# A kernel's head, written in a new order: local attention with a feed-forward layer on one Trainium2 core

## The chip, the core and the metric

The kernel runs on one core of a Trainium2 chip. The core has a matrix engine (TensorE, PE in the profile), three engines for element-wise work (VectorE or DVE, ScalarE or ACT, GpSimd or POOL) and SyncE (SP), which here only issues transfers. TensorE writes into PSUM, a small memory of banks, and VectorE and ScalarE read the banks out. Each engine works through its own instructions in order; semaphores tie the engines together. The metric is device microseconds of the whole program, less being better.

## The reference

q, k and v are 4 batches x 8 heads x 768 positions x 64. Each position attends to the 96 positions up to itself and to the first 8, with a bias that falls with distance; then a feed-forward layer with softplus follows.

```python
scores = scale * np.matmul(q, k.transpose(0, 1, 3, 2))
keep = is_global | is_local
bias = -slopes[:, None, None] * dist[None, :, :]
scores = np.where(keep, scores + bias[None], -1000000000.0)
a = np.exp(scores - np.max(scores, axis=-1, keepdims=True))
a = a / (np.sum(a, axis=-1, keepdims=True) + 1e-09)
x = np.matmul(a, v)      # then to 3072 x 512
h = x @ w_in             # 512 x 2048
g = np.maximum(h, 0.0) + np.log1p(np.exp(-np.abs(h)))
out = g @ w_out          # 2048 x 512
```

## The kernel before

**Tiling.** The 24 blocks of 128 queries are taken in units of two neighbouring blocks (`UNITS`, L175); a block sees its own keys and those of the block before it. Two blocks, 256 tokens, form a group of the feed-forward layer; there are 12 groups.

**A unit of attention** goes through named operations. In each name the first number is the unit or the block. `ldq`, `ldk`, `ldv` load (units 0 to 2 load q and k in two halves, `.0` and `.1`, L478); `castq`, `castk`, `castv` turn float32 into bfloat16 (L521 to L551; v in four pieces); `trq`, `trk` transpose q and k, on TensorE for units 0 to 2 (L629) and by a transposing DMA after that (L649, L658); `cpq`, `cpk` copy the transposed halves out of PSUM (L642). For a block n, `sc` makes the scores (L709, L764), on top of a bias that `sb` wrote for blocks 0 and 1, while for the others `z` adds the bias on VectorE (L790); `ex` takes the exponential on ScalarE (L795); `pv` multiplies by v (L821); `nm` divides by the sums on VectorE (L832, L833); `xt` transposes the result, by TensorE for blocks 0 to 5, with `xc` copying it into `XT` (L856, L861), and by a transposing DMA after that (L864). `gk` and `gv` copy the keys and values of the first 8 positions into the slots of the block before (L671, L680).

**A group of the feed-forward layer** has eight slots `a` g.0 to g.7 (`mm1`, L879; each is 8 matmuls of 128x256, and slots 2i and 2i+1 need the w_in pieces 2i and 2i+1), each followed by an exponential `e` on ScalarE (L896), and every two by a logarithm `ln` (L907), so that softplus is ln(1 + exp(h)). The even slots use PSUM bank h0, the odd ones h1. For groups 0 and 1 the second product is `b` g.ns.z (`mm2`, L927), two matmuls of 128x512 for each pair of the 16 rows blocks, with z from 0 to 14; `oc` copies it out and `st` stores it. From group 2 on a scheme of seven products with sums of tokens (`ka`) and of weights (`ws`, L354, on VectorE or GpSimd) replaces it.

**Weights.** `win` 0 to 7 and `wout` 0 to 7 load pieces of 512 KB, `cin` and `cout` cast them (L507). A cast that the code calls for any engine can be put on GpSimd, VectorE or ScalarE; what reads PSUM can be on VectorE or ScalarE.

**Buffers for loads.** There are 12 slots of raw data. They are given out in the fixed order of `FIRST_LOADS` (L178), whatever the order of issue: k0, q0, v0, q1, k1, v1, six pieces of w_in; then win7 takes the slot of k0, win6 that of q0, k2 that of v0, q2 that of q1, w_out 0 and 1 those of two w_in pieces, and so on. A load waits until the casts of what lay in its slot before are done, and behind it on SP's queue wait all later loads. From unit 3 on a load also waits for a slot of the feed-forward layer (L1268): q of unit 3 for a0.6, k for a1.0.

**The order.** It is written by hand in the string `ORDER` (L81): name, colon, engine (P, V, A, G, S), and after @ the PSUM home (s0 and s1 are of two banks, x, o, h0, h1 of one). `Program.in_order` (L63) emits the operations in just this order; so on each engine they stand in the order of the string, and everything else is waits that follow from what an operation reads and writes. A wait holds up all that stands behind it on that engine. `fill` 0 to 25 (L1024) are matmuls on a tile of zeros into bank x whose result nobody reads.

## Time and profile before

| | us |
|---|---|
| median of 3 runs | 210.27 |
| lowest and highest | 209.52, 210.4 |
| span of the profiled execution | 207.6 |
| median less that span | 2.7 |

The trace is of one execution; its span runs from the first to the last instruction. The profiled execution's own time is not given beside its span, so the 2.7 us are the distance to the median of the runs.

| stage of the trace, us | TensorE busy | VectorE | ScalarE | GpSimd | DMA share |
|---|---|---|---|---|---|
| 6.15 to 29.57 | 20.16 of 23.42 | 18.16 | 21.71 | 12.88 | 1.07 |
| 29.57 to 60.19 | 30.17 of 30.62 | 24.55 | 29.53 | 18.95 | 0.97 |
| 60.19 to 207.6 | 143.27 of 147.41 | 120.40 | 126.63 | 88.25 | 0.72 |

A row of a timeline has the start, the length, the engine, the line of the kernel, the instruction, what it writes and reads, the shapes and the number of instructions merged; brackets hold the idle time before it and what ended it. Matmuls are pipelined: the ends are modelled and overlap the next start, so a group's true share of TensorE is the distance of starts. SPq and ACTq are rows of a queue that issues transfers. A transfer's row has its size and the time from issue to landing.

### The profile page before, as it was taken

To read this page: it belongs to the slowest core of one execution; us is meant where nothing else is said; L and a number is where in the kernel's file an instruction comes from. 1 tells how busy PE (TensorE), PEld (TensorE's weight loads), DVE (VectorE), ACT (ScalarE), POOL (GpSimd) and SP (SyncE) were. 2 spreads that over 40 slices of the span, in tenths; PEclk is the share of its full clock that TensorE was granted. 3 is DMA by queue.
4 is the path that set the end of the run, shared out by engine and by line. 5 is a ranking of instruction groups with operands and counts; after the bars stand their busy time and mean duration, and the time that the engine had idled before them with its cause. 6 is when DMAs were issued, how large, how long until landed. Compare 5 with 4: busy or idle time off the path is not lost.

```text
span 207.6 us, 5574 instructions
## 1 busy us (share of the span) xinstructions
PE 198.6 (96%) x2174; PEld 161.1 (78%) x2174; DVE 166.3 (80%) x327; ACT 180.7 (87%) x271; POOL 123.3 (59%) x129
## 2 busy tenths in 40 slices
...
GB/s 185 345 347 384 393 370 364 258 229 190 293 134 245 190 239 242 252 228 231 205 196 224 204 94 229 148 139 244 218 190 27 129 87 33 0 53 102 52 74 133
DMA packets 69115, 41.00 MB, mean 198 GB/s; under 512 B 30432, under 2 KB 61664, under 8 KB 69088
## 3 DMA queue, kind: packets, MB, share of 16 engines
...
q8 instruction: 17, 0.28, 0.6%
...
## 4 chain that ended last, share of the span: by engine, by line
PE 74%; ACT 12%; DMA 8%; DVE 2%; issue 1%; ACTq 0%; SPq 0%; DVEq 0%
PE h_ps L879 24%; PE s_ps L417 12%; PE o_ps L417 9%; PE x_ps L417 5%; PE h_ps L1133 4%; DMA raw<-in_moe_w_in_dram 4%; PE s_ps L927 3%; PE s_ps L1133 3%; PE s_ps L764 3%; PE x_ps L821 3%; ACT e L896 3%; DMA XT<-xs 2%; ACT pb L795 2%; PE o_ps L927 2%; DMA raw<-in_q_dram 2%; ACT g L907 1%
## 5 line engine op out<-in xcount | busy, mean ns | idle before, releaser
L879 PE MATMUL h_ps<-XT,w_in_bf 128*128 128x256 bf16 x544 | 68.4, 273 | 1.4 <-DMA XT<-xs 0.6
L879 PEld LDWEIGHTS <-w_in_bf 128*128 128x128 bf16 x544 | 51.4, 98 | 10.4 <-issue 0.7
L790 DVE TENSOR_TENSOR z<-s_ps,biasA 128x1024 f32<-128x1024 f32 x38 | 45.7, 1217 | 3.7 <-PE s_ps L764 3.1
L896 ACT ACTIVATE e<-h_ps 128x512 f32<-128x512 f32 x68 | 42.1, 637 | 4.5 <-PE h_ps L879 3.9
L795 ACT ACTIVATE pb<-z 128x1024 bf16<-128x1024 f32 (+1 forms) x44 | 43.1, 994 | 2.6 <-DVE z L790 1.2
L907 ACT ACTIVATE g<-e 128x1024 bf16<-128x1024 f32 x34 | 35.0, 1053 | 0.3
L417 PEld LDWEIGHTS <-g 128*128 128x128 bf16 x320 | 30.8, 98 | 4.1
L417 PEld LDWEIGHTS <-raw 128*128 128x128 bf16 x240 | 23.3, 98 | 3.1 <-issue 0.3
L549 POOL CAST vb<-raw 64x512 bf16<-64x512 f32 x32 | 20.5, 640 | 5.3 <-DMA raw<-in_v_dram 3.3
L386 POOL TENSOR_TENSOR raw<-g,raw 128x1024 bf16<-128x1024 bf16 x8 | 17.9, 2232 | 5.6 <-DVE raw L386 5.3
L386 POOL TENSOR_TENSOR g<-g 128x1024 bf16<-128x1024 bf16 x5 | 11.6, 2312 | 11.3 <-DVE raw L386 11.1
L821 PEld LDWEIGHTS <-pb 128*128 128x128 bf16 x352 | 16.0, 97 | 2.6 <-ACT pb L795 0.8
L680 POOL COPY vb<-vb 4x512 bf16<-4x512 bf16 x15 | 9.3, 618 | 10.4 <-PE o_ps L821 5.9
L833 DVE TENSOR_TENSOR xs<-x_ps,rcp 128x256 bf16<-128x256 f32 x29 | 12.3, 424 | 1.0
L1193 ACT ACTIVATE g<-e 128x1024 bf16<-128x1024 f32 x12 | 12.6, 1053 | 0.2
L521 POOL CAST kb<-raw 128x1024 bf16<-128x1024 f32 x8 | 9.1, 1134 | 5.1 <-DMA raw<-in_k_dram 4.7
L530 POOL CAST qb<-raw 128x1024 bf16<-128x1024 f32 (+1 forms) x9 | 9.3, 1028 | 4.8 <-DMA raw<-in_q_dram 4.3
L821 PE MATMUL x_ps<-vb,pb 128*128 128x65 bf16 x220 | 11.6, 193 | 0.1
L1024 PE MATMUL x_ps<-blank 128*128 128x512 bf16 x26 | 9.8, 491 | 1.2 <-DVE blank L962 1.2
L417 PE MATMUL o_ps<-raw,g 128*128 128x256 bf16 x80 | 10.4, 273 | 0.0
L417 PE MATMUL s_ps<-raw,raw 128*128 128x256 bf16 x80 | 10.2, 273 | 0.0
L764 PE MATMUL s_ps<-qT,kT 64*128 64x128 bf16 x224 | 9.7, 217 | 0.3 <-DVE qT L636 0.3
(190 smaller groups left out, 396.8 us busy)
## 6 DMA issues: line engine op xcount, KB each, us to landing
raw<-in_v_dram SPq DMA_DIRECT2D x12, 512.0 KB, 5.9
out_dram<-osb SPq DMA_DIRECT2D x22, 256.0 KB, 2.7
raw<-in_q_dram SPq DMA_DIRECT2D x9, 512.0 KB, 5.8
raw<-in_k_dram SPq DMA_DIRECT2D x9, 512.0 KB, 4.7
raw<-in_moe_w_in_dram SPq DMA_DIRECT2D x8, 512.0 KB, 8.4
raw<-in_moe_w_out_dram SPq DMA_DIRECT2D x8, 512.0 KB, 7.8
raw<-in_k_dram SPq DMA_DIRECT2D x6, 256.0 KB, 4.7
raw<-in_q_dram SPq DMA_DIRECT2D x4, 256.0 KB, 5.5
```

What stands on the lines that cost most here:

```text
L386: (nc.vector if eng == "DVE" else nc.gpsimd).tensor_tensor(dst, a[0], b[0], ALU.subtract)
L417: nc.tensor.matmul(psum(j), lhs[:, f // 2, f % 2, :], w(f), start=(f == 0 and j in "125"), stop=(f == 7), skip_group_check=True,)
L549: copy_on[eng](dst, src)
L764: nc.tensor.matmul(reg if unit_of(n) in WIDE else reg.rearrange("p (r t) -> p r t", r=2), kt[rows, 2 * part + m, :], qv(rows, 2 * part + m ...
L790: op(f"z{n}.{part}", "DVE", lambda: nc.vector.tensor_tensor(z, scored(), bias, ALU.add), reads=b_keys(n, part) + key, writes=[("z", slot)] ...
L795: nc.scalar.activation(pb[:, 0:nr, :].rearrange("p (y a) b -> p y (a b)", y=2), scored() if n in PE_BIAS else z, AF.Exp, scale=1.0 / root_d,)
L821: nc.tensor.matmul(xv[:, h, :], pb[:, 4 * (h % 2) + 2 * part + h // 2 if lone else u_all * (2 * (h % 2) + h // 2) + u, :], vb_of(prev if u ...
L879: last = nc.tensor.matmul(hv[:, j, :], w_in_bf[:, m, fb * P : fb * P + P], XT[g % NXG][:, m, :], start=(m == 0), stop=(m == NM - 1),)
L896: nc.scalar.activation(e[:, p % 2, :, :].rearrange("p j (b t r) -> p (j b) r t", b=2, r=2), hb[:].rearrange("p (a r t) -> p a r t", a=4, r=2),
L907: nc.scalar.activation(gt[:, 2 * p - 2 : 2 * p + 2, :].rearrange("p a t -> p (a t)"), e[:].rearrange("p a j t -> p (a j t)"), AF.Ln, bias=1.0,
L1133: nc.tensor.matmul(bank(sess[j])[:, W * f : W * f + W], F[j][:, m, P * f : P * f + P], X[j][0][:, m, :], start=(m == 0 and j in "15"), sto ...
L1193: nc.scalar.activation(gt[:, 4 * i : 4 * i + 4, :].rearrange("p a t -> p (a t)"), flat(e), AF.Ln, bias=1.0,)
```

## The change

Only the string `ORDER` changes, and only its first 366 of 1147 words: from the beginning up to `castk5.0`, just ahead of the words `e2.5`, `b1.1.4`, `nm7.0`, `sc8.0`. Behind that, all words, engines and PSUM homes are the same, on other lines of the string. The words are the same set in both: no operation is added or removed. The number of operations by engine in this head goes from 116 to 116 on TensorE, 88 to 75 on ScalarE (with the two loads of q0 that it issues), 77 to 88 on VectorE, 42 to 44 on GpSimd, and 43 to 43 on SP.

Of the moves between engines: `cin7`, `cout0`, `cout4`, `cout5`, `castk3.0`, and seven pieces of v go from GpSimd to VectorE; `castq3.0`, `xc2`, `xc4`, `xc5`, `cout3` from ScalarE to VectorE; `cin1`, `cout6`, `ws0.5`, `ws0.7`, `ws1.7`, `ws2.5`, `ws2.7`, `ws2.4`, `ws3.7` from VectorE to GpSimd; `xc1`, `cpq0.0`, `cpq2.1`, `oc0.0.0`, `oc1.0.0` from VectorE to ScalarE; `cin3` from GpSimd to ScalarE.

The order of the loads that SP issues begins, before, with k0.0, k0.1, q1.1, v0, k1.0, q1.0, k1.1, v1, win1, k2.0, win0, k2.1, q2.0, win3, q2.1, win2, win5, win4, win6, win7, wout0, v2, wout4. After, it begins with k1.0, k0.1, k0.0, k1.1, v0, win3, q1.1, q1.0, win0, k2.1, win1, q2.0, v1, k2.0, win2, q2.1, win5, win4, win6, win7, v2, wout2, wout0. ScalarE issues q0's halves, in the other order after.

The removed lines up to the point where the orders meet, and then the added ones:

```diff
--- before.py
+++ after.py
@@ -79,63 +79,63 @@
 
 ENGINES = {"P": "PE", "V": "DVE", "A": "ACT", "G": "POOL", "S": "SP"}
 ORDER = """
-ldk0.0:S ldq0.0:A blank:V ident32:G fill11:P@x ldk0.1:S ldq0.1:A fill22:P@x iota:G fill21:P@x ldq1.1:S table:A
-fill19:P@x dl1a:V ldv0:S fill15:P@x dl0a:V ldk1.0:S dl0b:V fill4:P@x dl1c:V fill0:P@x dl0c:V ldq1.0:S d0:V fill17:P@x
-d0e:V ldk1.1:S fill18:P@x biasF5:V biasF1:A biasF6:G castq0.0:A fill3:P@x ldv1:S fill6:P@x biasF2:V fill24:P@x dl1e:V
-castk0.0:A ident:G castk0.1:V biasA4:A ones:G trk0.0:P@s0 castq0.1:A biasA5:V biasF7:G cpk0.0:A trq0.0:P@s1 biasF4:V
-biasA1:V biasF3:A fill1:P@x biasF0:A biasA6:V fill14:P@x biasA2:A cpq0.0:V fill23:P@x win1:S cpk0.1:A fill7:P@x
-sb0.0:P@h0+h1 biasA3:A cpq0.1:A castv0.00:V biasA7:A castv0.11:G sc0.0:P castv0.01:A biasA0:V sb1.1:P@s1 castv0.10:G
-ex0.1:A sc1.1:P castq1.0:V ex0.0:A ldk2.0:S sb1.0:P@s0 castk1.0:G ex1.1:A fill8:P@x castk1.1:V win0:S sc1.0:P
-castq1.1:V ldk2.1:S fill9:P@x ex1.0:A trk1.0:P@s1 ldq2.0:S pv0.0:P@o fill12:P@x nm0.0:V castv1.00:A win3:S trq1.0:P@s0
-ldq2.1:S cpk1.1:V pv1.0:P@h0 cpq1.0:A fill16:P@x pv0.1:P@h1 win2:S fill5:P@x cpq1.1:A nm0.1:V fill10:P@x win5:S
-cpk1.0:A castk2.0:G nm1.0:V win4:S sc2.0:P@s1+s0 win6:S castv1.01:G fill13:P@x win7:S z2.0:V pv1.1:P@h0 cin0:G z2.1:V
-sc3.0:P@s1 ex2.0:A fill20:P@x nm1.1:V gv4.1:A xt0:P@h1 castv1.10:G fill2:P@x castk2.1:A z3.0:V xt1:P@h0 castv1.11:G
-xc0:A trk2.0:P@s0 castq2.0:A pv2.0:P@h1 cin1:V sc3.1:P@s1 cpk2.1:A cin3:G xc1:V wout0:S ex3.0:A nm2.0:V a0.0:P@h0
-ldv2:S z3.1:V castq2.1:G ex2.1:A a0.1:P@h1 e0.0:A cin2:V pv3.0:P@o e0.1:A fill25:P@x trq2.0:P@s1 gv4.0:V ex3.1:A
-cin5:G a0.2:P@h0 cpq2.0:V ln0.0:A nm3.0:V pv3.1:P@x wout4:S gk4:G a0.3:P@h1 cin4:G nm3.1:V wout1:S gk8:A cpk2.0:A
-wout2:S cpq2.1:V pv2.1:P@o e0.3:A wout3:S nm2.1:V sc4.0:P@s0+s1 e0.2:A z4.0:V ln0.1:A gk5:G xt2:P@h0 cin6:G xt3:P@x
-a0.5:P@h1 xc2:A xc3:V z4.1:V cin7:G a0.4:P@h0 e0.5:A ex4.0:A sc5.0:P@s0 cout0:G sc5.1:P@s1 z5.0:V e0.4:A a0.7:P@h1
-castv2.00:G ln0.2:A z5.1:V a0.6:P@h0 e0.7:A cout4:G e0.6:A ldq3:S a1.1:P@h1 wout5:S castv2.01:V ex4.1:A cout1:G
-a1.0:P@h0 e1.1:A pv4.0:P@o e1.0:A pv4.1:P@x cout2:G nm4.0:V b0.1.0:P@s1 gv5.1:A a1.2:P@h0 castv2.10:A ws0.5:V ln1.0:A
-b0.0.0:P@s0 gv5.0:G nm4.1:V a1.3:P@h1 castv2.11:V e1.2:A ws0.7:V ldk3:S xt4:P@x e1.3:A b0.1.2:P wout7:S ws1.7:V
-b0.0.2:P ex5.1:A wout6:S a1.4:P@h0 ws0.6:V cout5:G b1.0.0:P@o e1.4:A a1.5:P@h1 cout3:A ws1.5:V b1.0.2:P ws2.5:V e1.5:A
-b0.1.4:P ws0.4:V b0.0.4:P ex5.0:A a1.7:P@h1 castk3.0:G ln1.1:A a1.6:P@h0 ws2.7:V xc4:A cout7:G ldk4:S b1.0.4:P ln1.2:A
-ldv3:S b0.0.6:P ws1.6:V pv5.1:P@x trk3.0:S b0.1.6:P ln0.3:A nm5.1:V b0.1.8:P ws2.6:V b0.1.10:P e1.6:A b1.0.6:P cout6:V
-castq3.0:A pv5.0:P@x b0.0.8:P nm5.0:V b0.0.10:P e1.7:A trq3:S ws1.4:V b1.0.8:P ln1.3:A b0.0.12:P castk4.0:G b1.0.10:P
-trk3.1:S xt5:P@x ws3.7:V b0.1.12:P xc5:A b0.0.14:P ws3.5:G gv6.1:A ldq4:S b1.0.12:P oc0.0.0:V castv3.10:A b0.1.14:P
-trk4.0:S a2.0:P@h0 gk6:A ws2.4:V oc0.1.0:A castv3.00:G sc6.0:P@s0+s1 ldv4:S e2.0:A ws3.6:G z6.0:V castv3.01:A
-a2.2:P@h0 z6.1:V gv6.0:G a2.1:P@h1 e2.2:A ldk5:S castv3.11:G gk7:A ex6.0:A b1.0.14:P gv8.0:V castq4.0:G sc7.0:P@s1+s0
-oc1.0.0:V e2.1:A a2.4:P@h0 z7.0:V ex6.1:A trq4:S a2.3:P@h1 e2.4:A z7.1:V trk4.1:S pv6.0:P@x e2.3:A pv6.1:P@o a2.6:P@h0
-gv7.1:G nm6.1:V gv7.0:A ex7.1:A nm6.0:V a2.5:P@h1 castv4.00:G castv4.01:V xt6:S ex7.0:A gv8.1:G pv7.1:P@x b1.1.0:P@o
-nm7.1:V castv4.10:G b1.1.2:P e2.6:A ldq5:S pv7.0:P@x castk5.0:G e2.5:A b1.1.4:P nm7.0:V sc8.0:P@s0+s1 ln2.1:A xt7:S
...
+ldq0.1:A ident32:G blank:V iota:G fill11:P@x ldk1.0:S dl1a:V fill4:P@x ldq0.0:A fill9:P@x dl0a:V dl0b:V table:A
+fill1:P@x dl0c:V ident:V d0:G d0e:V ldk0.1:S dl1c:V fill3:P@x fill13:P@x castq0.1:A biasF5:G biasF0:G dl1e:V biasA7:A
+ldk0.0:S fill10:P@x biasA1:V fill21:P@x biasF3:A fill16:P@x fill8:P@x fill24:P@x castq0.0:A fill20:P@x ldk1.1:S
+castk0.0:A biasF4:V biasA2:V ldv0:S trq0.0:P@s1 castk0.1:G biasF7:V cpq0.0:A cpq0.1:V biasF1:V win3:S fill6:P@x
+biasA3:A biasF2:V ldq1.1:S ldq1.0:S biasF6:V biasA6:V castk1.1:V trk0.0:P@s0 cpk0.1:A fill7:P@x sb0.0:P@h0+h1 biasA4:V
+castk1.0:G fill23:P@x fill17:P@x trk1.0:P@s1 biasA5:A castv0.11:V cpk0.0:A cpk1.1:V biasA0:G sc0.0:P castv0.00:G
+sb1.0:P@s0 cpk1.0:A castv0.01:V castv0.10:V ex0.1:A ex0.0:A fill19:P@x ones:G win0:S sb1.1:P@s1 ldk2.1:S sc1.1:P
+fill14:P@x pv0.1:P@o ex1.1:A win1:S nm0.1:V castq1.0:G cin0:G pv0.0:P@h0 sc1.0:P nm0.0:V fill25:P@x fill5:P@x ldq2.0:S
+ldv1:S ldk2.0:S pv1.1:P@x nm1.1:V castq1.1:A cin1:G ex1.0:A castv1.01:G trq1.0:P@s1 win2:S cpq1.0:A xt0:P@o pv1.0:P@h1
+cpq1.1:V xc0:A sc2.0:P@s1+s0 fill18:P@x fill22:P@x nm1.0:V z2.0:V cin3:A xt1:P@o castv1.11:G xc1:A fill0:P@x
+castk2.0:G z2.1:V castk2.1:V ex2.1:A sc3.1:P@s1 sc3.0:P@s0 ex2.0:A z3.0:V castv1.00:V a0.0:P@h0 ex3.0:A ldq2.1:S
+e0.0:A win5:S castq2.0:G fill12:P@x fill2:P@x z3.1:V pv2.1:P@o castq2.1:G cin5:G cin2:V gk8:A a0.1:P@h1 win4:S nm2.1:V
+e0.1:A pv2.0:P@h0 win6:S castv1.10:V fill15:P@x trk2.0:P@s0 ex3.1:A a0.3:P@h1 cpk2.1:A nm2.0:V pv3.1:P@o e0.3:A
+nm3.1:V trq2.0:P@s1 a0.2:P@h0 cpk2.0:A cpq2.0:V pv3.0:P@h1 win7:S xt2:P@o cin4:G cpq2.1:A gk4:A e0.2:A cin6:G
+sc4.0:P@s0+s1 ln0.1:A nm3.0:V xt3:P@x ldv2:S a0.4:P@h0 ln0.0:A gv4.0:V gk5:V z4.1:V a0.5:P@h1 e0.4:A wout2:S
+sc5.1:P@s1 cin7:V xc2:V wout0:S xc3:V e0.5:A a0.6:P@h0 z4.0:V castv2.10:V ex4.1:A a0.7:P@h1 ws1.5:V e0.6:A wout1:S
+gv4.1:G e0.7:A sc5.0:P@s0 castv2.00:G ex4.0:A a1.0:P@h0 castv2.01:G z5.0:V cout2:G e1.0:A ws0.5:G a1.1:P@h1 gk6:V
+cout0:V wout3:S wout4:S pv4.0:P@o wout6:S z5.1:V e1.1:A a1.2:P@h0 a1.3:P@h1 cout1:G ex5.0:A e1.2:A ws0.6:V ldq3:S
+castv2.11:G pv4.1:P@x wout5:S ldk3:S cout3:V b0.0.0:P@s0 ln0.2:A e1.3:A ws0.4:V b0.1.0:P@s1 gv5.1:V b0.0.2:P nm4.0:V
+b0.0.4:P wout7:S ws0.7:G b0.1.2:P b0.0.6:P cout4:V ex5.1:A ws1.7:G gv5.0:A ln0.3:A a1.4:P@h0 ws1.6:V b0.1.4:P ws2.5:G
+cout6:G e1.4:A nm4.1:V a1.5:P@h1 ws1.4:V pv5.0:P@o b0.1.6:P nm5.0:V ldv3:S castq3.0:V e1.5:A b0.1.8:P ln1.0:A cout7:G
+xt4:P@h1 b0.0.8:P xc4:V a1.6:P@h0 pv5.1:P@o trq3:S cout5:V ln1.2:A e1.6:A a1.7:P@h1 b0.1.10:P ws2.7:G gv8.1:V nm5.1:V
+b1.0.0:P@x castk3.0:V xt5:P@h0 b0.1.12:P e1.7:A xc5:V ws3.5:G trk3.0:S trk3.1:S b0.0.10:P ln1.1:A castv3.00:V
+a2.1:P@h1 b0.0.12:P gv8.0:V b0.0.14:P ldq4:S b1.0.2:P oc0.0.0:A ws2.6:V gv6.1:V gv6.0:A castv3.01:V b0.1.14:P
+a2.0:P@h0 oc0.1.0:A sc6.0:P@s0+s1 castv3.10:G b1.0.4:P ws2.4:G ln1.3:A e2.1:A z6.0:V gk7:V b1.0.6:P e2.0:A ex6.0:A
+z6.1:V b1.0.8:P castv3.11:V castq4.0:G b1.0.10:P a2.2:P@h0 ex6.1:A ldk4:S pv6.0:P@o sc7.0:P@s1+s0 castk4.0:G e2.2:A
+nm6.0:V z7.1:V a2.3:P@h1 ldv4:S pv6.1:P@o gv7.1:G ex7.1:A b1.0.12:P b1.0.14:P gv7.0:G a2.4:P@h0 oc1.0.0:A nm6.1:V
+ws3.7:G ldk5:S b1.1.0:P@o z7.0:V b1.1.2:P pv7.1:P@x e2.4:A castv4.01:G trq4:S trk4.0:S ws3.6:G e2.3:A castv4.00:V
+trk4.1:S a2.6:P@h0 xt6:S ex7.0:A nm7.1:V a2.5:P@h1 e2.6:A castv4.10:V ldq5:S pv7.0:P@x castk5.0:G e2.5:A b1.1.4:P
+nm7.0:V sc8.0:P@s0+s1 ln2.1:A xt7:S ta0.3:G b1.1.6:P z8.1:V ln2.0:A a2.7:P@h1 st0.0.0:S z8.0:V b1.1.8:P ex8.1:A ldv5:S
...
```

55 lines of the change are left out of this document (27 added, 28 removed).

## The prediction

> **What bounds the kernel now.** I read the page first, then the busy times by stage, the chain of waits, the DMA issues, and last the timelines of the single engines in the stretch that the change rewrites.
>
> ```profile
> span 207.6 us, 5574 instructions
> ...
> PE 198.6 (96%) x2174; PEld 161.1 (78%) x2174; DVE 166.3 (80%) x327; ACT 180.7 (87%) x271; POOL 123.3 (59%) x129
> ```
>
> TensorE is busy for 96% of the span, so time can only come from where it waits. Stages (columns: PE, PEld, DVE, ACT, POOL busy; clock; DMA share; GB/s), cut at the seventh feed-forward slot of group 0 and where pv7.0 ends, the last matmul group whose place changes:
>
> ```profile
> 6.15:29.57 23.42, 20.16 (x263) 14.28 (x262) 18.16 (x41) 21.71 (x40) 12.88 (x18) 1.00 1.07 367
> 29.57:60.19 30.62, 30.17 (x297) 21.51 (x294) 24.55 (x40) 29.53 (x45) 18.95 (x21) 1.00 0.97 263
> 60.19:207.60 147.41, 143.27 (x1613) 123.63 (x1609) 120.40 (x233) 126.63 (x186) 88.25 (x81) 1.00 0.72 156
> ```
>
> From 29.57 to 60.19 TensorE idles 30.62 - 30.17 = 0.45 us. Ahead of that it idles 3.26 us, and 14 of the 26 fillers stand there, matmuls whose result nobody uses. So the head up to 29.57 is where time lies, and beyond it nearly none. What holds the head is in the chain of waits (start, length, what) and the DMA busy tenths of the first 40 us, one digit per us:
>
> ```profile
> 14.28 8.05 DMA raw<-in_moe_w_in_dram
> ...
> 22.35 0.70 DVE w_in_bf L507
> ...
> 23.10 1.05 PE h_ps L879 x8
> ```
>
> ```profile
> DMA  0069999999999999999999999999999999998369
> ```
>
> The transfers run without a pause from 3 to 36 us, and the chain goes through a w_in piece, its cast, and the feed-forward slot that needed it. The head is bound by loading. The last w_in piece is win7; its issue and its time to landing:
>
> ```profile
> 17.00 0.42 SPq L506 DMA_DIRECT2D raw<-in_moe_w_in_dram  x1
> ...
> raw<-in_moe_w_in_dram SPq DMA_DIRECT2D x1, 512.0 KB, 10.7
> ```
>
> It lands at 17.00 + 10.7 = 27.7 us. No slot a0.6 or a0.7 can run ahead of that in either order.
>
> **The change part by part.** *Loads.* The new order shuffles the loads, but the set that stands ahead of win7 on the queue is the same in both: q, k and v of units 0 and 1, q and k of unit 2, and eight w_in pieces. The stream has no pause to remove, so win7 still lands at about 27.7.
>
> *Cast of win7.* It moves from GpSimd to VectorE, whose cast of such a piece is here, with the slot that it released:
>
> ```profile
> 22.35 0.69 DVE L507 CAST w_in_bf<-raw 128x1024 bf16<-128x1024 f32 x1 [0.77 <-DMA raw<-in_moe_w_in_dram]
> ...
> 23.10 1.05 PE L879 MATMUL h_ps<-XT,w_in_bf 128*128 128x256 bf16 x8 [0.19 <-DVE w_in_bf L507]
> ```
>
> So a0.6 starts at S = 27.7 + 0.05 + 0.69 + 0.06 = 28.5. TensorE is there by then: what is ordered ahead of a0.6 is what before does ahead of 29.57, without sc5.0; with the 3.26 us of idling taken out it would be through at 26.3. On VectorE the copies xc2 and xc3 and the addition z4.0 queue behind this cast, and sc5.0 needs the bank that z4.0 reads:
>
> ```profile
> 17.75 1.21 DVE L790 TENSOR_TENSOR z<-s_ps,biasA 128x1024 f32<-128x1024 f32 x1
> ...
> 18.89 0.68 DVE L507 CAST w_in_bf<-raw 128x1024 bf16<-128x1024 f32 x1
> ...
> 19.48 0.42 DVE L861 COPY XT<-h_ps 128x512 bf16<-128x512 bf16 x1
> ...
> 19.82 0.17 DVE L832 RECIPROCAL rcp<-h_ps 128x4 f32<-128x4 f32 x1
> ```
>
> By the starts, a cast takes 0.59 of the queue and a copy 0.34. The cast starts at 27.75, the copies at 28.3 and 28.7, z4.0 at 29.0, and it ends at 30.2. sc5.0 is due after a0.6 and a0.7, at 28.5 + 1.75 = 30.25. It fits with nothing to spare; each us by which z4.0 is later costs one.
>
> *What TensorE has left from a0.6.* Before, rows of TensorE's timeline from the sc5 groups and a0.7 on:
>
> ```profile
> 29.02 0.62 PE L764 MATMUL s_ps<-qT,kT 64*128 64x128 bf16 x16
> ...
> 29.57 1.92 PE L879 MATMUL h_ps<-XT,w_in_bf 128*128 128x256 bf16 x16
> ...
> 31.78 1.91 PE L879 MATMUL h_ps<-XT,w_in_bf 128*128 128x256 bf16 x16 [0.29 <-ACT e L896]
> ...
> 33.52 0.41 PE L821 MATMUL o_ps<-vb,pb 128*128 128x65 bf16 x8
> ...
> 59.94 0.40 PE L821 MATMUL x_ps<-vb,pb 128*128 128x65 bf16 x8
> ...
> 60.17 0.59 PE L927 MATMUL o_ps<-w_out_bf,g 128*128 128x512 bf16 x2
> ```
>
> From 29.57 to 60.17 are 30.60 us, with both slots a0.7 and a0.6 in them. Out go the idle 0.45 and another 0.17 that the modelled ends hide: two slots take 33.52 - 31.78 = 1.74, but 31.78 - 29.57 = 2.21 passed, and only 0.29 of the 0.47 lost is shown. In comes sc5.0, half of the two groups at 29.02: 0.28. That leaves 30.3 us. New waits: I keep 0.3, one like the 0.29 for ScalarE above; the bounds are 0 and 1.3 (behind all of before's 0.45, the tight place at sc5.0, and b0.1.10, which waits for cout5 and so for a late load).
>
> *The other moves.* ScalarE, 29.53 of 30.62 busy, gets 75 operations in the rewritten head instead of 88; VectorE goes from 77 to 88 and GpSimd from 42 to 44. Relief of ScalarE costs or gives nothing as long as TensorE is the bound; it lowers the chance of more 0.29 waits. Fillers are as many as before and run while data is awaited: nothing. New PSUM homes of pv, xt and of transposed q and k only order who waits for whom ahead of a0.6, which has two us of room: nothing. On VectorE castv2.10 and ws1.5 now wait for v2 and w_out 2, the two loads right after win7, ahead of z5.0; behind them queue z5.0, cout0, z5.1. The page's second part has the rate in 40 slices:
>
> ```profile
> GB/s 185 345 347 384 393 370 364 258 229 190 293 134 245 190 239 242 252 228 231 205 196 224 204 94 229 148 139 244 218 190 27 129 87 33 0 53 102 52 74 133
> ```
>
> At the 345 to 393 GB/s of the head a load of 512 KB takes 1.3 to 1.5 us, so w_out 2 is there by 31, and pv5.0, which wants z5.0's result, is ordered nine feed-forward slots and six pairs after a0.6 begins. Nothing, unless loads slip by more than three us.
>
> *Sum.* pv7.0 is through at 28.5 + 30.3 + 0.3 = 59.1 instead of 60.17: 1.1 us. Behind it the order is word for word the same, and TensorE is the bound, so the 1.1 us reach the end. The span becomes 206.5; the runs' median 210.27 lies 2.7 above the profiled span, which makes 209.2.
>
> **The rivals.** *The load queue runs dry: no change.* win0 to win7 come in time only if SP issues in time. A load waits until its buffer was read, and SP issues in order:
>
> ```profile
> 6.35 1.24 SPq L506 DMA_DIRECT2D raw<-in_moe_w_in_dram  x1
> ...
> 10.52 0.55 SPq L473 DMA_DIRECT2D raw<-in_k_dram  x1
> ...
> 9.02 1.47 POOL L549 CAST vb<-raw 64x512 bf16<-64x512 f32 x2 [2.58 <-DMA raw<-in_v_dram]
> ...
> raw<-in_moe_w_in_dram SPq DMA_DIRECT2D x1, 512.0 KB, 7.7
> ...
> raw<-in_k_dram SPq DMA_DIRECT2D x1, 256.0 KB, 3.5
> ```
>
> Before, k2's first half waited until GpSimd had cast v0 (9.02 + 1.47), and the load ahead of it landed at 6.35 + 7.7 = 14.1. The new order has the same wait at ldk2.1, and the last cast of v0 stands on VectorE behind two other casts and a copy of k1's transpose, which need TensorE's trk1.0:
>
> ```profile
> 6.97 0.62 PE L627 MATMUL s_ps<-ident,qb 128*128 128x128 bf16 x8 [0.21 <-ACT qb L530]
> ...
> 8.92 0.42 DVE L549 CAST vb<-raw 64x512 bf16<-64x512 f32 x1 [0.60 <-DMA raw<-in_v_dram]
> ...
> 13.75 0.68 DVE L636 COPY kTa<-s_ps 128x512 bf16<-128x512 bf16 x1
> ```
>
> Before, q0 and k0 were transposed by 6.97 + 0.62 = 7.6. k0's first half is now SP's third load, not its first, so this comes one load of 256 KB, 0.7 us, later: 8.3. Then five operations of VectorE (four biases and a cast, none over 0.5) and trk1.0 itself, some 2 us; then 0.68 + 2 x 0.42. My estimate for the issue of ldk2.1 is 12.0. With the 3.5 us of a load on an empty queue it lands at 15.5, while the stream would have brought it at 14.1 + 0.7 = 14.8. The gap lies between 0 (earlier loads still move) and 1.0 us, and all of it comes back at win7. With 1.0 the gain is 0.1: 210.2. It decides from about 0.5 us on.
>
> *VectorE and GpSimd hold each other up: slower.* Place: VectorE's chain of 23 operations from castv2.10 to xc5, which a2.1 waits for. Its sums of weights (L354) take 0.68 alone, and 1.52 beside a cast on GpSimd:
>
> ```profile
> 38.59 1.28 DVE L354 TENSOR_TENSOR raw<-raw 128x512 bf16<-128x512 f32 x2
> ...
> 39.79 3.56 DVE L354 TENSOR_TENSOR raw<-raw,raw 128x512 bf16<-128x512 f32 x3
> ...
> 39.26 1.51 POOL L507 CAST w_out_bf<-raw 128x1024 bf16<-128x1024 f32 x1 [2.34 <-DMA raw<-in_moe_w_out_dram]
> ...
> 43.55 1.04 POOL L507 CAST w_out_bf<-raw 128x1024 bf16<-128x1024 f32 x1 [1.34 <-DMA raw<-in_moe_w_out_dram]
> ```
>
> Three sums in 3.56 instead of 1.9, and a cast of 1.51 instead of 1.04. Before, only 1 us of such meetings lay in this stretch for GpSimd's casts; after, GpSimd itself makes five of the sums there (ws0.5, 0.7, 1.7, 2.5, 2.7) while VectorE makes ws0.6, 0.4, 1.6 and 1.4. At 0.84 each, four meetings cost 3.4 us. The chain has some 1.0 us of room against TensorE's need, so a2.1 would wait 2.4, and the result is 1.3 later than before: 211.6. It makes the kernel slower once VectorE loses more than 2.1 us there. Against it: before, VectorE met the casts from 38.6 to 43.35 and TensorE did not wait. By the Trainium skill (SBUF - State Buffer, Who interferes with whom) a VectorE instruction with two SBUF inputs and a GpSimd instruction that reads SBUF exclude each other for a whole instruction; the trace's 1.52 beside 0.68 agrees, and by that rule the new order invites such meetings.
>
> *The clock drops: slower.* With the fillers used up early, TensorE may idle up to 2 us between a0.5 and a0.6; its longest wait in the head so far is the 0.64 below. The first fillers show half speed:
>
> ```profile
> 1.17 5.14 PE L1024 MATMUL x_ps<-blank 128*128 128x512 bf16 x12 [1.17 <-DVE blank L962]
> ...
> 7.43 1.03 PE L1024 MATMUL x_ps<-blank 128*128 128x512 bf16 x4
> ...
> 15.60 0.40 PE L764 MATMUL s_ps<-qT,kTa 64*128 64x128 bf16 x8 [0.64 <-ACT kTa L636]
> ```
>
> Twelve took 0.43 each, the later four at most 0.26. Five us at half speed again would lose 2.5: 211.7. It needs a longer pause than I expect. The Trainium skill (TensorE: Matmul & The Clock Gate, What's actually happening) puts the idle window that halves the clock at about 3.4 us; no row here shows a pause of that length.
>
> *The gain is lost later: no change.* Behind pv7.0 a3.1 waits for a transposing DMA, and such waits could take up the lead:
>
> ```profile
> 66.24 1.92 PE L879 MATMUL h_ps<-XT,w_in_bf 128*128 128x256 bf16 x16 [0.56 <-DMA XT<-xs]
> ```
>
> 0.5 to 1 us of the lead would go: 210.0. Against it: that DMA's issue moves with the lead too.
>
> **How the numbers follow.** A measurement of this kernel can tell about 0.5%, 1.05 us, from no change, so faster means under 209.2 and slower over 211.3. Chances: forecast 0.53 (own range 208.5 to 209.8, from S between 28.2 and 28.9 and new waits from 0 to 0.6; 0.40 of it under 209.2), dry queue 0.17, lost later 0.07, hold-ups 0.17, clock 0.06. Faster 0.40; same 0.13 + 0.17 + 0.07 = 0.37; slower 0.23. The range reaches from the forecast's lower end, 208.5, to the hold-ups' 211.6, and leaves out some 0.05 below and 0.14 above.
>
> **What would show it.** Right: the DMA digits show no pause up to 36 us; win7 lands at 27.7; the feed-forward slot after the second sc5 half's z starts at 28.5; pv7.0 ends near 59.1; behind it each matmul group lies 1.1 us earlier. Dry queue: a digit under 9 near 13 us and win7 past 28.5. Hold-ups: L354 on DVE with means over 1.0 us, and an idle time of TensorE that xc5 (DVE XT L861) ends near 44 us. Clock: feed-forward slots of 1.7 us after 28. I am wrong altogether if TensorE waits between 30 and 58 us for something not named here, or if the stretch behind pv7.0 takes other than 147.4 us.

## The result, and the profile after

The new order makes the kernel slower. Its median is 219.10 us (218.63 to 219.74, 4 runs) beside 210.34 for the kernel before (209.52 to 211.35, 4 runs): a ratio of 1.0417, 95% interval 1.0379 to 1.0455. The ratios of this document leave out runs that are over 1.5% longer than the shortest of their kernel (in e3, e7 and e11), while the medians are over all runs. The profiled execution took 219.23 us, its span 217.2. From the page of the new kernel:

```profile
span 217.2 us, 5586 instructions
...
PE 201.0 (93%) x2174; PEld 162.0 (75%) x2174; DVE 175.9 (81%) x338; ACT 174.6 (80%) x258; POOL 131.2 (60%) x131
...
PEclk9999699999999999999999999999999999999999
```

TensorE has the same 2174 matmuls, yet it idles 16.2 us instead of 9.0, and one slice of the clock row, near 25 us, has a 6. The stages, cut at a0.6 and behind pv7.0 (columns as before):

```profile
0.00:33.58 33.58, 26.35 (x267) 16.60 (x268) 23.18 (x57) 22.13 (x38) 17.08 (x29) 0.95 0.89 300
33.58:68.90 35.32, 31.43 (x301) 21.90 (x301) 32.56 (x49) 25.89 (x37) 24.17 (x22) 1.00 0.81 218
68.90:217.20 148.30, 143.23 (x1611) 123.53 (x1607) 120.12 (x234) 126.61 (x185) 89.90 (x82) 1.00 0.69 156
```

a0.6 starts at 33.58, forecast was 28.5. From there until pv7.0 is through at 68.80 it takes 35.2 us, forecast was 30.6. Behind that, 148.3 instead of 147.4. In the middle stage VectorE is now busier than TensorE, 32.56 of 35.32 us beside 31.43; before it was busy for 24.55 of 30.62.

**The head.** The view of the transfers from 5 to 36 us (40 digits, 0.775 us each, and their GB/s), first before, then after:

```profile
DMA  9999999999999999999999999999999999999999
GB/s 333 330 324 354 340 398 347 311 317 365 383 381 351 312 354 383 407 386 396 399 402 399 383 386 394 388 396 399 326 330 353 387 396 402 412 423 366 287 318 367
```

```profile
DMA  9999999999002899779999999999999999999999
GB/s 370 367 353 333 326 316 320 389 404 378 32 0 45 299 354 248 216 182 252 279 357 392 403 375 354 402 394 404 399 389 355 326 328 363 389 412 391 407 412 396
```

The stream stops from 12.75 to 15.1 us, and for five us more it runs at 182 to 354 GB/s. Over the ten slices from 12.75 the rates add up to 3752 before and 1907 after; the difference times 0.775 is 1430 KB, 3.7 us of a full stream. SP's queue and VectorE's timeline in the new kernel show who stopped it:

```profile
6.05 0.59 SPq L506 DMA_DIRECT2D raw<-in_moe_w_in_dram  x1
13.39 0.54 SPq L473 DMA_DIRECT2D raw<-in_k_dram  x1
...
15.26 0.59 SPq L482 DMA_DIRECT2D raw<-in_v_dram  x1
```

```profile
10.65 0.65 DVE L549 CAST vb<-raw 64x512 bf16<-64x512 f32 x1
11.33 0.69 DVE L636 COPY kTa<-s_ps 128x512 bf16<-128x512 bf16 x1
12.05 1.27 DVE L549 CAST vb<-raw 64x512 bf16<-64x512 f32 x2
```

ldk2.1 waits from 6.6 to 13.39, until the last cast of v0 ends at 13.32, as the first rival said. Behind it stands v1, issued at 15.26. The chain of waits goes on from there:

```profile
15.26 7.76 DMA raw<-in_v_dram
23.14 0.81 POOL vb L549
23.99 0.38 PE o_ps L821 x4
24.37 1.71 PE h_ps L879 x8
```

and TensorE's timeline shows what the wait did:

```profile
20.70 0.59 PE L1024 MATMUL x_ps<-blank 128*128 128x512 bf16 x2
23.99 0.38 PE L821 MATMUL o_ps<-vb,pb 128*128 128x65 bf16 x4 [2.69 <-POOL vb L549]
24.18 1.89 PE L879 MATMUL h_ps<-XT,w_in_bf 128*128 128x256 bf16 x8
25.87 0.42 PE L821 MATMUL h_ps<-vb,pb 128*128 128x65 bf16 x4
```

After 2.69 us without a matmul the slot a0.1 takes 25.87 - 24.18 = 1.69 us, about twice the 0.87 between slots elsewhere. From 24 to 26 us the granted clock was 0.50. Of the 26 fillers 25 stood ahead of the wait and were used up. From v1 on the chain leads through TensorE to z4.1, on VectorE at 31.59, and through the cast of win7 behind that to a0.6. By the prediction's own terms win7's landing, at 31.16, would have let a0.6 start at 31.16 + 0.05 + 0.69 + 0.06 = 31.96, an estimate; the other 1.6 us to 33.58 come from this chain.

**The rest.** What TensorE waited for from 33.6 to 70 us:

```profile
PE h_ps L856 <- DVE xs L833: 1.2, 1, 1.2
PE h_ps L879 <- DVE XT L861: 1.1, 1, 1.1
PE o_ps L821 <- DVE xs L833: 0.6, 1, 0.6
PE s_ps L927 <- DVE z L790: 0.5, 1, 0.5
PE s_ps L927 <- DVE w_out_bf L507: 0.4, 1, 0.4
```

All five are VectorE's; the only other one is 0.2 us for a DMA. Its timeline, and GpSimd's beside it:

```profile
40.88 0.68 DVE L354 TENSOR_TENSOR raw<-raw,raw 128x512 bf16<-128x512 f32 x1
41.48 1.76 DVE L507 CAST w_out_bf<-raw 128x1024 bf16<-128x1024 f32 x1
43.17 1.75 DVE L354 TENSOR_TENSOR raw<-raw,raw 128x512 bf16<-128x512 f32 x1
```

```profile
39.29 3.41 POOL L354 TENSOR_TENSOR raw<-raw,raw 128x512 bf16<-128x512 f32 x2
42.77 1.60 POOL L354 TENSOR_TENSOR raw<-raw 128x512 bf16<-128x512 f32 x1
```

While GpSimd makes ws0.7, ws1.7 and ws2.5, VectorE's cast cout3 and its sum ws0.4 take 1.76 and 1.75 instead of 0.68. The sum ws0.6, at 40.88 between GpSimd's ws0.7 and ws1.7, takes 0.68. Longer than 0.68 are also ws1.5 (1.65), ws1.6 (1.52), ws1.4 (1.20) and castq3.0 (1.21). Together these six take 9.1 where 6 x 0.68 = 4.1 would be: 5.0 us of VectorE's time.

### The profile page after: what moved, and what is told of

The parts are those of the page before. It is cut to its first block, busy times and chain, and to the rows that moved or that the text cites. A ratio compares the mean times of both kernels' runs of the same rounds, so it can differ in the third digit from the quotient of the medians.

```text
span 217.2 us, 5586 instructions
## 1 busy us (share of the span) xinstructions
PE 201.0 (93%) x2174; PEld 162.0 (75%) x2174; DVE 175.9 (81%) x338; ACT 174.6 (80%) x258; POOL 131.2 (60%) x131
## 4 chain that ended last, share of the span: by engine, by line
PE 59%; DMA 15%; DVE 13%; ACT 6%; issue 3%; SPq 1%; POOL 1%; ACTq 1%; DVEq 0%; POOLq 0%
PE h_ps L879 17%; PE s_ps L417 11%; PE o_ps L417 9%; DMA raw<-in_v_dram 7%; PE x_ps L417 5%; PE h_ps L1133 4%; DMA raw<-in_moe_w_in_dram 3%; PE s_ps L764 3%; PE s_ps L1133 3%; DVE raw L354 3%; DMA XT<-xs 2%; DMA raw<-in_q_dram 2%; PE x_ps L821 2%; DVE z L790 2%; DVE w_out_bf L507 2%
## 5 line engine op out<-in xcount | busy, mean ns | idle before, releaser
L879 PE MATMUL h_ps<-XT,w_in_bf 128*128 128x256 bf16 x544 | 69.7, 275 | 2.7 <-DMA XT<-xs 1.3
L879 PEld LDWEIGHTS <-w_in_bf 128*128 128x128 bf16 x544 | 51.5, 98 | 12.0 <-DMA XT<-xs 1.4
L896 ACT ACTIVATE e<-h_ps 128x512 f32<-128x512 f32 x68 | 42.3, 635 | 13.2 <-PE h_ps L879 12.8
L530 POOL CAST qb<-raw 128x1024 bf16<-128x1024 f32 (+1 forms) x11 | 10.5, 958 | 10.4 <-DMA raw<-in_q_dram 10.0
L354 POOL TENSOR_TENSOR raw<-raw,raw 128x512 bf16<-128x512 f32 x7 | 9.7, 1385 | 4.3 <-DVE raw L354 3.8
L549 DVE CAST vb<-raw 64x512 bf16<-64x512 f32 x13 | 9.9, 764 | 2.5 <-DMA raw<-in_v_dram 2.2
L833 DVE TENSOR_TENSOR xs<-x_ps,rcp 128x256 bf16<-128x256 f32 x26 | 11.0, 425 | 0.9
L821 PE MATMUL x_ps<-vb,pb 128*128 128x65 bf16 x196 | 10.4, 193 | 0.1
```

The lines of the kernel that those rows point to most:

```text
L354: (nc.vector if eng == "DVE" else nc.gpsimd).tensor_tensor(dst, a, b, fn)
L549: copy_on[eng](dst, src)
L821: nc.tensor.matmul(xv[:, h, :], pb[:, 4 * (h % 2) + 2 * part + h // 2 if lone else u_all * (2 * (h % 2) + h // 2) + u, :], vb_of(prev if u ...
L879: last = nc.tensor.matmul(hv[:, j, :], w_in_bf[:, m, fb * P : fb * P + P], XT[g % NXG][:, m, :], start=(m == 0), stop=(m == NM - 1),)
L896: nc.scalar.activation(e[:, p % 2, :, :].rearrange("p j (b t r) -> p (j b) r t", b=2, r=2), hb[:].rearrange("p (a r t) -> p a r t", a=4, r=2),
```

## The experiments

Theory A: two causes. The load queue runs dry (head), and VectorE and GpSimd hold each other up (rest). Theory B: in the rest it is the order on VectorE's queue, whoever makes the sums. Theory C: the halved clock behind the 2.69 us wait. The other letters are explained where they come. In the table, "over before" is the ratio to the kernel before on the same chip, less 1, with its 95% interval. The last three columns are of the profiled execution: the start of the first of a0.6 and a0.7, the start of the group behind pv7.0, and the us between them, which I call the rest.

| kernel | median, us | over before, % | slots from | pv7.0 through | rest |
|---|---|---|---|---|---|
| before | 210.34 | | 29.57 | 60.17 | 30.6 |
| the new order | 219.10 | 4.2 (3.8 to 4.6) | 33.58 | 68.80 | 35.2 |
| e1_loads | 216.45 | 2.6 (2.3 to 3.0) | 29.98 | 65.73 | 35.8 |
| e2_small_sums | 214.99 | 1.9 (1.5 to 2.4) | 31.48 | 64.84 | 33.4 |
| e3_loads_small_sums | 213.81 | 1.1 (0.7 to 1.5) | 29.77 | 60.91 | 31.1 |
| e4_more_fillers | 217.91 | 3.3 (3.0 to 3.6) | 31.72 | 68.54 | 36.8 |
| e5_engines_back | 217.87 | 3.5 (2.8 to 4.1) | 34.95 | 68.37 | 33.4 |
| e6_before_sums_gpsimd | 214.84 | 2.2 (1.6 to 2.7) | 29.91 | 64.01 | 34.1 |
| e7_loads_engines_back | 214.38 | 1.7 (1.1 to 2.2) | 29.42 | 63.08 | 33.7 |
| e8_v0_casts_off_vector | 218.86 | 3.8 (3.2 to 4.4) | 29.79 | 65.84 | 36.1 |
| e9_new_head_old_rest | 215.74 | 2.3 (1.8 to 2.9) | 35.42 | 67.24 | 31.8 |
| e10_old_head_new_rest | 217.81 | 3.6 (3.0 to 4.2) | 30.24 | 66.79 | 36.6 |
| e11_mended_head_old_rest | 213.07 | 1.0 (0.7 to 1.3) | 31.52 | 62.12 | 30.6 |
| e12_mended_joint | 212.42 | 1.0 (0.6 to 1.4) | 30.18 | 61.93 | 31.8 |
| e13_old_head_late_sum | 218.37 | 3.9 (3.4 to 4.4) | 30.82 | 67.33 | 36.5 |
| e14_old_head_new_rest_small | 214.80 | 2.1 (1.8 to 2.4) | 31.11 | 63.94 | 32.8 |
| e15_old_head_small_late | 215.64 | 2.2 (1.4 to 3.0) | 31.00 | 64.86 | 33.9 |

Several of these kernels scatter by 2 to 4.7 us between runs, and the profiled execution is one of them: it is the shortest of its kernel in e3 (211.51), e7 (213.18) and e8 (216.91), the longest in e1 (218.15) and e9 (217.29). Times are judged by the intervals, the traces by what they show inside. The new order, e2 and e5 have the same words, engines and loads ahead of a0.6, and yet it starts at 33.58, 31.48 and 34.95; so a difference of two us in the column "slots from" shows nothing by itself.

### The two causes

**e1**, the order of four loads:

```diff
-win0:S ... ldk2.1:S ... win1:S ... ldq2.0:S ldv1:S
+win0:S ... win1:S ... ldv1:S ... ldk2.1:S ldq2.0:S
```

> The changed order with one thing made anew: on SP, win1 and ldv1 come ahead of ldk2.1, so that the queue has work while ldk2.1 waits for v0's casts. Theory A (two causes: the load queue runs dry ahead of ldk2.1, and later VectorE and GpSimd hold each other up): win7 lands near 28 instead of 31.2, a0.6 starts two to three us earlier, and the time falls by 2 to 3.5 us, to some 216 to 217; the hold-ups stay. Theory B (the load pause is hidden, VectorE's queue between a0.6 and a2.1 alone sets the end): the time stays at 219. Theory C (the halved clock after TensorE's wait of 2.7 us costs): the wait moves with the loads, a0.1 takes 0.87 and the time falls by 1.

The same view of the transfers for e1:

```profile
DMA  9999999999999999999999999999999999999999
```

ldk2.1 still goes out only at 13.19, but two loads are in front of it and the stream has no pause. a0.6 starts at 29.98 instead of 33.58, pv7.0 is 3.1 us earlier, and 1.6 points of the 4.2 are gone. In the rest VectorE's stretched operations are as long as before (ws1.5 1.68, cout3 1.77, ws0.4 1.75).

**e2**, GpSimd's sums cut short; they add 8 of 256 columns, and the kernel leaves out the others:

```diff
 def ex(eng, dst=dst, a=a, b=b, fn=fn):
+    if eng != "DVE":
+        nc.gpsimd.memset(dst, 0.0)
+        dst, a, b = dst[:, :, 0:8], a[:, :, 0:8], b[:, :, 0:8]
```

> The changed order, in which each sum of weights that stands on GpSimd writes zeros and adds only 8 of 256 columns, so it hardly reads SBUF (that part of the computation is left out; VectorE's sums are whole). Theory A: VectorE's sums and casts between 35 and 55 us go back from 1.2 to 1.8 us to 0.7, a2.1 comes some 4 us earlier, and the time falls to some 215. Theory B (VectorE's queue is late through its order and late loads, not through hold-ups): durations may fall but the time stays within 1 us of 219. Theory C: 219.

VectorE's sums with two operands, from 31 to 69 us, by line, for the new kernel's order with short sums:

```profile
L357 DVE TENSOR_TENSOR raw<-raw,raw 128x512 bf16<-128x512 f32 x5 | 3.4, 681 | 0.0
```

The same five had a mean of 1166 ns in the new kernel. VectorE's casts of w_out stay long (mean 1193 ns, 972 in the new kernel). 2.3 points are gone and pv7.0 is 4.0 us earlier, but only 1.9 us of these lie in the rest (33.4 instead of 35.2). The other 2.1 lie in the head, which the edit doesn't touch: in this execution v1 was there earlier, pv2.1 waited 1.83 us, and the slot a0.1 had its full speed:

```profile
22.42 0.29 PE L824 MATMUL o_ps<-vb,pb 128*128 128x65 bf16 x4 [1.83 <-POOL vb L552]
22.55 1.03 PE L882 MATMUL h_ps<-XT,w_in_bf 128*128 128x256 bf16 x8
23.42 0.29 PE L824 MATMUL h_ps<-vb,pb 128*128 128x65 bf16 x4
```

**e3**, both edits.

> Both edits together: loads in the other order, and GpSimd's sums of weights cut to 8 columns (left out). Theory A: both gains add, 7 to 8 us, to some 211 to 212. Theory B: as without the load edit. If the prediction's sum was right but for these two terms, 209 to 210.

3.1 points of the 4.2 are gone. The rest takes 31.1 us; with the loads alone it took 35.8, with the short sums alone 33.4. So in the rest the loads come to count only when the sums are short. Theory A holds for most of the loss, as far as the places go: the loads, and GpSimd's sums. What is left is 1.1% (0.7 to 1.5). The profiled execution (211.51 us) is the shortest of ten; its span of 209.5 is 1.9 over before's 207.6, and of these 0.2 lie ahead of the slots, 0.5 in the rest and 1.2 behind pv7.0, where TensorE waits 1.3 us for a transposing DMA instead of 0.6. The median is 2.3 us longer still, and no trace shows why.

**e4**, twelve more fillers ahead of pv2.1, against theory C:

```diff
-FILLERS = 26
+FILLERS = 38
-... pv2.1:P@o
+... fill26:P@x ... fill37:P@x pv2.1:P@o
```

> The changed order with 12 more fillers on TensorE ahead of pv2.1, where it waits 2.7 us for v1 and its clock halves. Theory C: a0.1 takes 0.87 instead of 1.7 and the time falls by about 1 us, to 218. Theories A and B: a0.1 is faster but a0.6 waits for win7 all the same: 219, no change.

```profile
20.22 3.19 PE L1025 MATMUL x_ps<-blank 128*128 128x512 bf16 x14
23.24 0.29 PE L822 MATMUL o_ps<-vb,pb 128*128 128x65 bf16 x4
23.37 1.03 PE L880 MATMUL h_ps<-XT,w_in_bf 128*128 128x256 bf16 x8
24.24 0.29 PE L822 MATMUL h_ps<-vb,pb 128*128 128x65 bf16 x4
```

With TensorE kept busy through the wait, a0.1 takes 0.87 again: that pause and half speed go together is shown. What the half speed costs in time isn't. a0.6 starts at 31.72 instead of 33.58, but in this execution the loads were early too: ldk2.1 went out at 12.90 instead of 13.39, and v1 and win7 landed 1.2 us earlier. The head of e2, with no added fillers, reaches a0.6 at 31.48. The time falls by 0.9 points, while pv7.0 comes at 68.54 instead of 68.80: the rest takes 36.8 us behind the earlier head. And the new order's own runs don't follow the clock. In the one whose mean granted clock was 1.00 it took 218.97, in those with 0.992, 0.984 and 0.983 it took 219.23, 219.74 and 218.63. In e1 they do: 215.91 to 216.54 in four runs at 1.00, 218.02 and 218.15 in two at 0.992. So theory C's mechanism is there, and its share of the 4.2 points stays open.

### The sums alone, and the engines put back

**e6**, one part of the change in the kernel before:

```diff
-ws0.5:V ws0.7:V ws1.7:V ws2.5:V ws2.7:V
+ws0.5:G ws0.7:G ws1.7:G ws2.5:G ws2.7:G
```

> The kernel before with one part of the change alone: ws0.5, ws0.7, ws1.7, ws2.5 and ws2.7 on GpSimd at the places that they hold in the order of before; nothing else is changed. VectorE has 5 x 0.68 = 3.4 us less to do. Theory A: GpSimd's sums take 1.2 to 1.7 each and stretch the sums and casts beside them on VectorE to 1.2 to 1.7, GpSimd's casts of w_out behind them come later, a2.0 is 2 to 4 us later and the time is 212 to 215. Theory B: with VectorE relieved nothing is later, 210 to 211. The head up to 29.57 is as before in both.

2.2%, 4 us, from five sums on another engine, though VectorE has less to do. VectorE's and GpSimd's timelines:

```profile
39.22 3.45 DVE L354 TENSOR_TENSOR raw<-raw,raw 128x512 bf16<-128x512 f32 x2
```

```profile
38.83 3.29 POOL L354 TENSOR_TENSOR raw<-raw,raw 128x512 bf16<-128x512 f32 x2
```

Each such sum takes 1.6 to 1.8 on both engines. What TensorE ends up waiting for, in its timeline, is something else:

```profile
55.13 0.62 PE L764 MATMUL s_ps<-qT,kT 64*128 64x128 bf16 x16 [2.97 <-DMA qT<-qb]
```

What held up SP is in the waits of its queue from 36 to 56 us, and the sum that ended this wait in GpSimd's timeline:

```profile
SPq L482 <- POOL raw L354: 8.5, 1, 8.5
```

```profile
46.10 1.61 POOL L354 TENSOR_TENSOR raw<-raw,raw 128x512 bf16<-128x512 f32 x1
```

This is ws2.7. The load of k4 needs the buffer that it reads, and goes out at 47.73, when the sum is done; before, VectorE was done with ws2.7 at 42.75 and the load went out at 42.89. Behind it on SP's queue stand the transposes of unit 3 (48.79 instead of 43.99 for the first), and sc6.0 waits 2.97 us. For VectorE TensorE waits 0.5 us in this stretch. Theory A's size is right; the way to TensorE is through GpSimd's late sum and then SP's queue, which neither theory had named.

**e5**, the new order with the engines of before behind the head, and **e7**, the same with the loads of e1. Edit (23 words, those that the expectation names):

```diff
-ws0.5:G ws0.7:G ... cout0:V cout3:V ... castq3.0:V xc4:V xc5:V
+ws0.5:V ws0.7:V ... cout0:G cout3:A ... castq3.0:A xc4:A xc5:A
```

> The new order, word for word at its new places, but the operations behind the head have the engines of the kernel before: the sums of weights ws0.5, 0.7, 1.7, 2.5, 2.7, 2.4 and 3.7 back on VectorE; cout0, cout4, cout5 and castk3.0 back on GpSimd, cout6 on VectorE; cout3, castq3.0, xc4 and xc5 on ScalarE; the pieces of v of units 2 and 3 as before. The loads and everything ahead of a0.6 are as in the new kernel. Theory A (VectorE and GpSimd hold each other up when both have sums with two inputs): VectorE's sums go back to means under 0.9, a0.6 stays at 33.6, pv7.0 ends 31 to 32 us later, near 65, and the time is 215 (214 to 216). Theory B (the order of VectorE's queue is what delays TensorE, whoever makes the sums): pv7.0 stays near 68.5 and the time within 1 of 219.

> Both remedies in a kernel that computes everything: SP's order win1, ldv1, ldk2.1, ldq2.0 (as in the run of the loads alone) and the engines of before behind the head. Theory A: a0.6 at 30.0, pv7.0 ends near 61, the time is 211.5 (210.5 to 212.5); what is left over before is the head, whose a0.6 is still 0.4 later than the first of the two last slots was before. Theory B: 216 (215.5 to 217), as with the loads alone.

e5 misses theory A's 215 (217.87), e7 its 211.5 (214.38). In e5's profiled execution pv2.1 waited 3.41 us, two slots were slow (1.69 and 1.70 us) and a0.6 came at 34.95. From there the rest takes 33.4 us, and 33.7 in e7: shorter than the new order's 35.2, longer than theory A's 31 to 32. Loads mended, the engines of before bring 2.6 - 1.7 = 0.9 points, less than the sums cut short do (1.5). In e7's middle (28 to 66 us) TensorE waits for another engine:

```profile
PE h_ps L879 <- ACT e L896: 1.0, 2, 0.5
PE h_ps L856 <- ACT e L896: 1.0, 1, 1.0
```

VectorE's waits are down to 0.2 and ScalarE, which has its casts and copies back at places chosen without them, is late. Neither theory's sizes are met; engines and places belong together.

**e8**, the casts of v0 off VectorE, the loads as in the new order:

```diff
-cpk0.0:A ... castv0.00:G ... castv0.01:V castv0.10:V
+cpk0.0:A castv0.01:A ... castv0.00:G castv0.10:G
```

> The new kernel with castv0.01 on ScalarE, behind cpk0.0, and castv0.10 on GpSimd, behind castv0.00, as the kernel before has them; the order of the loads stays the new one. So ldk2.1 no longer waits for VectorE's copy and casts. Theory A1 (the dry queue came from the late issue of ldk2.1): it is issued at 11.3 to 11.8 instead of 13.4, every load behind it and win7 land 1.5 to 2 us earlier (win7 at 29.2 to 29.7), pv2.1 waits 0.7 to 1.2 instead of 2.7, a0.6 starts at 31 to 32, and the time is 217 (216.3 to 217.8). Rival A2 (the late places of v1 and win1 among the loads do it, whenever ldk2.1 is issued): v1 still lands near 23, the wait stays over 2 us, and the time is within 0.7 of 219.

In the profiled execution ldk2.1 goes out at 11.23, win7 at 19.66 instead of 21.58, pv2.1 waits 0.8 and a0.6 starts at 29.8, earlier than A1 says. That run took 216.91 us; the three others took 218.81 to 219.18, and the median is inside A2's range. The trace speaks for A1, the time leaves it undecided. The mean granted clock, 0.999 in that run, doesn't sort the runs: 218.92 came with 0.998.

### The two halves of the change

The string was cut at the first of a0.6 and a0.7; what one half lacks comes from the other kernel, in its order.

> The two halves of the change taken apart. Up to the first of the slots a0.6 and a0.7 the new order; behind that everything in the order, on the engines and in the PSUM homes of the kernel before. Theory A (two causes that add: the new head loses by its loads, the new rest by VectorE and GpSimd holding each other up): the rest starts near 33.5 and takes 31 us, pv7.0 ends at 64 to 65.5, the time is 215 (214 to 216). Rival D (it is the late loads alone, w_out and v of unit 2 among them, and any rest behind such a head is slow): pv7.0 near 68 and the time within 1.5 of 219.

> The other half: up to a0.7 the order, the engines and the loads of the kernel before, behind that the new order. Theory A: the rest starts at 29.6 and takes 34 to 35.5 us, with VectorE's sums of 1.2 to 1.8, pv7.0 ends at 64 to 65, the time is 215 (213.5 to 216). Rival D (late loads alone): the rest takes 30.6 to 31.5 and the time is 210.5 to 211.5.

New head, old rest: 2.3%, inside theory A's range for the time, but 2.00 us of it are made by the joint, where sc5.0, now ahead of a0.7, waits for z4.0, pv7.0 misses A's 64 to 65.5, and in all four runs the mean granted clock was 0.992. Old head, new rest: 3.6%; theory A's 215 (213.5 to 216) is exceeded by 1.8 us. Rival D falls: the new rest is slow behind the old head, with its loads in time. And the halves don't add: behind the old head the new rest takes from 30.24 to 66.79, 36.6 us, behind the new one 35.2. It ends only 2.0 us earlier for a start 3.3 us earlier.

**e13**, **e14** and **e15** ask what the new rest waits for behind the old head: ws1.5 moved behind z5.1; GpSimd's sums cut as in e2; both.

```diff
-castv2.10:V ws1.5:V ... z5.0:V ... z5.1:V
+castv2.10:V ... z5.0:V ... z5.1:V ws1.5:V
```

> The old head with the new rest, and the sum ws1.5 behind z5.1 on VectorE instead of ahead of z5.0, so that z5.0, cout0 and z5.1 no longer queue behind the load of w_out that it waits for. Theory B (order on VectorE's queue): 2.5 to 3.4 us come back, pv7.0 ends near 63.7 and the time is 214.5 to 215.3. Theory A (hold-ups by GpSimd's sums): the wait is absorbed by what follows; at most 1 us comes back, 216.8 to 218.

> The old head with the new rest, GpSimd's sums of weights cut to 8 of their 256 columns (what they leave out is set to zero), so that they take a fraction of the time and hardly meet VectorE. Theory A: 4 us or more come back, pv7.0 ends at 61.5 to 63, the time is 212 to 214. Theory B: VectorE still waits 3.4 us for the load of w_out and the time is 216 to 218.

> The old head with the new rest, GpSimd's sums cut to 8 of 256 columns (what they leave out is zero), and ws1.5 behind z5.1. If the two are two limits of one chain (whichever is slower sets the time), both removed give more than the two alone: TensorE's wait of 1.3 us for z5.1 goes, and with it 1.3 to 2.5 us against the run with the short sums, 212.3 to 213.5. If the order on VectorE's queue is worth nothing, 214.8 as with the short sums alone.

TensorE's largest wait from 30 to 66 us in each:

```profile
PE s_ps L927 <- POOL w_out_bf L507: 2.4, 1, 2.4
```

```profile
PE s_ps L930 <- DVE z L793: 1.3, 1, 1.3
```

```profile
PE s_ps L930 <- POOL w_out_bf L510: 1.8, 1, 1.8
```

Moving ws1.5 gives nothing, against theory B; the short sums give 1.5 points, 3.0 us, less than A's 4 us; both together give no more. GpSimd's timeline in e15 has the reason:

```profile
35.55 1.56 POOL L510 CAST w_out_bf<-raw 128x1024 bf16<-128x1024 f32 x1 [2.29 <-DMA raw<-in_moe_w_out_dram]
...
37.95 1.56 POOL L510 CAST w_out_bf<-raw 128x1024 bf16<-128x1024 f32 x1
```

The first of these casts is cout2, whose piece lands at 35.43. The second is cout1, which b0.0.2 waits for until 39.56. Its piece is there from 34.15, but GpSimd waits for piece 2 first. The old head loads w_out 1 ahead of 2, the new rest casts 2 ahead of 1. So a third limit lies under the other two, and 2.2% stay.

### Is the new head worth anything?

**e11**: the new head with the edits of e1 and e8, and the old rest. **e12**: the joint set right too.

```diff
-z4.1:V ... cin7:V xc2:V xc3:V ... sc5.0:P@s0 ... z5.0:V ... a0.7:P@h1 ... z5.1:V a0.6:P@h0
+z4.1:V z4.0:V xc2:V xc3:V ... cin7:G ... a0.7:P@h1 ... z5.1:V a0.6:P@h0 sc5.0:P@s0 z5.0:V
```

> The new head with its loads mended both ways (SP's order win1, ldv1, ldk2.1, ldq2.0; castv0.01 on ScalarE and castv0.10 on GpSimd, so that ldk2.1 goes out by 11.5), and the rest of the kernel before. Theory A: the slots start near 29.5, pv7.0 ends at 60 to 61 and the time is 210.5 (209.5 to 211.5), the same as before. Rival E (the new head is slower in itself, by its order on TensorE, whatever its loads do): the slots start after 30.5 and the time is 212 or more.

> The mended new head with the rest of the kernel before, and the joint of the two set right: z4.0 directly behind z4.1 on VectorE, ahead of xc2 and xc3; cin7 on GpSimd; sc5.0 and z5.0 behind a0.6 instead of ahead of a0.7. Theory A (the loss was the loads, and the wait of 2.0 at the joint): the two last slots start at 29.0 to 29.5, pv7.0 ends at 59.5 to 60.5, the time is 210.0 (209.3 to 211.0). Rival E (the new head loses by itself): 212 to 213, as with the joint's wait.

Both are 1.0% slower than before. In e12 the first of the two slots starts at 30.18 instead of 29.57, and from 28 to 63 us TensorE waits 1.7 us in three places for ScalarE (PE h_ps L879, ACT e L896). pv7.0 is through 1.8 us later than before. Rival E's size is met: mended, the new head gains nothing. No version found beats the kernel before.

## Why the prediction was wrong, point by point

- **"The stream has no pause to remove, so win7 still lands at about 27.7."** This step failed first. The set of loads ahead of win7 is the same; their order and the time of issue are not. The first rival had the mechanism and the place, and mis-sized two terms. ldk2.1 went out at 13.39, not 12.0: between the copies of q0's and k1's transposes VectorE had seven operations, not five, among them a bias of 0.70 and the cast castv0.11 of 0.65, and the two casts behind the copy took 1.27 instead of 0.84. And the gap was bounded at 1.0, the pause alone; the stream also needed five us to be full again, and win7 came 3.4 later, at 31.16. With two loads ahead of ldk2.1 (e1) the pause is gone, and with it 1.6 of the 4.2 points. The chance of 0.17 was too low for a wait that the code shows.
- **"TensorE is there by then ... at 26.3."** The order of v1 on SP's queue was not followed: from eighth place to thirteenth, behind ldk2.1, win1 and ldq2.0. pv2.1 then waits 2.69 us for v1's cast, and TensorE reaches a0.6 at 33.45. So both terms of S = 28.5 were wrong, and it came out as 33.58. The 3.26 us of idling were taken out whole, and no new waits were put in their place.
- **The cast of win7.** It started at 32.74, behind z4.1 on VectorE (31.59 + 1.23), not 0.05 after the landing. TensorE, late itself, waited only 0.13 us for it: the step was incomplete, its price here small.
- **The clock (0.06).** It fell in a pause of 2.69 us without a matmul, where I had asked for a longer one, and not between a0.5 and a0.6 but ahead of a0.1. The Trainium skill (TensorE: Matmul & The Clock Gate, What's actually happening) has the clock halved after an idle window of about 3.4 us; in this trace a shorter pause was enough, and the measurement decides. What it costs in time is not shown: e4 falls by 0.9 points, but the new order without the fall in clock took no less (218.97).
- **"New waits: I keep 0.3 ... the bounds are 0 and 1.3."** The rest took 35.2 us instead of 30.6. The rival named the place and the mechanism, and was wrong in the count: it priced four sums at 0.84, 3.4 us. Casts were stretched too, cout3 by 1.08 and castq3.0 by 0.53, and the six operations lost 5.0. It also called the chain's room 1.0 us, while the change had moved four casts of w_out onto VectorE and one off it. The wait that it named came further ahead in the chain: a1.7 waits 1.06 us for xc4, at 52.40, where it had a2.1 wait for xc5. The Trainium skill (SBUF - State Buffer, Who interferes with whom) counts a VectorE instruction in a two-port mode with those that exclude GpSimd; cout3's 1.76 beside 0.68 agrees, if the cast runs in such a mode, which no run here shows.
- **"Against it: before, VectorE met the casts ... and TensorE did not wait."** In e6 VectorE's stretched sums hardly hold up TensorE either (0.5 us), and yet five sums on GpSimd cost 2.2%, by GpSimd's own lateness. The argument looked at VectorE alone and left that way out.
- **"Relief of ScalarE costs or gives nothing."** No gain is seen, with ScalarE busy for 25.89 of 35.32 us. It was paid for on VectorE.
- **"Behind pv7.0 the same."** Nearly: 148.3 instead of 147.4 us, with 1.3 of waiting for the transposing DMA instead of 0.6.
- **Small slips that change nothing.** pv5.0 is ordered eight slots and seven pairs after a0.6 begins, not nine and six. The own range, worked out from its two terms, is 208.6 to 209.9.

Shares: the loads alone are worth 1.6 points of the 4.2, the sums alone 2.3 beside the new order (with a luckier head in the trace) and 1.5 in the two other pairs (e1 and e3, e10 and e14), both together 3.1. The clock's share is open, and no run brought the loss to zero. Whether GpSimd's sums hurt more by stretching VectorE or by holding up GpSimd's own queue, e2 does not separate, since it shortens both; in e6 it was GpSimd's own lateness.
